# A planned schedule for windowed attention and two feed-forward networks: more word buffers, another cost model in the planner, other ranks

## The chip, the cores and the metric

One core of one Trainium2 chip runs the whole program in one launch. The metric is device time in microseconds (us), lower is better. The engines are TensorE (PE in the profile, PEld its weight loads), VectorE (DVE), ScalarE (ACT), GpSimd (POOL) and SyncE (SP), which issues nearly all transfers in program order.

## The reference

Inputs are float32. There are three parts, each fed by the one before:

```python
# attention: batch 4, 8 heads, 576 positions, head_dim 64
scores = q @ k^T / 8 - slope[head] * |i - j|      # only 0 <= i - j < 128
x = softmax(scores) @ v                           # -> 2304 tokens x 512
# first network: 512 -> 1024 -> 512
h = x @ w_in
solu = h * softmax(h)
ln = (solu - mean) / sqrt(var + 1e-6) * g_ln
x = ln @ w_out
# second network: 512 -> 1536 -> 512
g, val = x @ w_gate, x @ w_val
out = (g * sigmoid(g) * val) @ w_out2
```

## The kernel before, in words

**Attention** goes through 20 steps c (4 batches, 5 blocks of 128 query positions, the last of 64). A step has four units of two heads each. `load(c)` (line 380) fetches queries, keys and values; `score(c, qd)` (line 437) forms the scores of two units as small tiled products (line 463); `attend(u)` (line 484) adds the bias on VectorE (line 504), takes exponentials on ScalarE (lines 530 and 539), turns the result on TensorE (line 558), copies it to SBUF (lines 568 and 571) and multiplies it with the values, again as small tiled products (line 607). For steps c below `SUMS` (4, line 49) the division by the row sums comes after the product with the values: small products of the inverse sums with the identity (line 615) spread them, ScalarE or VectorE copies them (line 637), VectorE multiplies (line 640). For later steps each unit is normalized before it is turned (`invert`, lines 508 to 510, and `normalize`, lines 512 to 517). For steps below `WHOLE` (20, line 51) the products with the values come in two groups of two units, otherwise in one group of four (line 577).

**The first network** works on 18 tiles of 128 tokens: `up(i)` (line 716) is 24 products of 512 columns (line 712) and the statistics, `flip(i)` (line 778) turns the normed tile, and `down1(i)` (line 830) is another 24 products (line 712). For tiles in `FLIP_BY_DMA` (4 to 13, line 47) the turn is done by transfers: a copy splits the words in 16-bit halves (`halves_of`, line 261), a store writes them to memory and a turning transfer brings them back (line 258). Other tiles are turned by 8 TensorE transposes (line 817). Four buffers `e1` hold the exponentials until the turn is done.

**Weights** come as 64-bit words. `fetch` (line 289) takes one of the `DEC1[0]` = 4 buffers `dw` (line 38) and loads 512 KB; `unpack` (line 303) makes float32 of it with two ScalarE operations (lines 311 and 315), two VectorE operations (316 and 317) and an add on GpSimd (319), which gives the buffer back (line 321). Then the value is split in a high and a low part, and every dense product is the sum of three such products. `w_in` has 8 blocks, `w_out` 8. The second network has 36 more (`DEC2`).

**The second network** runs 36 steps of seven products (`products(s)`, line 1064, products in line 1083), in an order mostly written out by hand (`line`, lines 872 to 883), then the last product (`steps_of(k)`, line 1241, products in line 1262).

**The planner.** All of this is written as generators that yield operations. `Emitter.run` (line 199) plays them against a cost model and so fixes the program order of every engine: at each turn it takes the earliest time at which an engine can start an operation, and among that engine's operations that are ready at that time the one of lowest rank (lines 206 to 217). An operation with several ways (engines) goes where its end, plus a bias for VectorE and ScalarE (line 82), comes first. Ranks count tiles: a step's is its first token over 128, its loads come 0.5 earlier (line 1321), the up-projection of tile i has i + `LEAD`, the down-projection i + `LEAD` + `R_DOWN`; `PW_IN` and `PW_OUT` are ranks of the weight blocks, the `O_` constants offsets of single operations. What `dma` returns as its fifth entry is the time from the end of the issue to the landing (lines 254 to 259). For TensorE there is a rule on tiled operations (`form` 1 for scores, 2 for values, 0 for all else):

```python
if ops[0][4][0] == "PE" and first > TOGETHER:
    tiled = [x for x in ops if form(x)]
    if 0 < len(tiled) < len(ops) and not self.form:
        if len(tiled) < LEAST and min(x[3][2] for x in tiled) > first - PATIENCE:
            ops = [x for x in ops if not form(x)]
    elif tiled and self.form:
        same = [x for x in tiled if form(x) == self.form]
        ops = same or tiled
```

Here `first` is the time that can be had, `x[3][2]` the time at which an operation became ready, and `TOGETHER` 76077.562 ns. The planner's costs and dependences choose order and engine only; on the chip an instruction waits for the data and buffers that it uses.

Of the kernel before, what the change touches and what calls it, by code (L numbers as in the profile page):

```python
# [13 lines left out]
AF = mybir.ActivationFunctionType  # L14
# [7 lines left out]
DF1 = 1024  # L22
# [15 lines left out]
DEC1 = (4, 2)  # L38
# [8 lines left out]
FLIP_BY_DMA = range(4, 14)  # L47
PLB = 2
SUMS = 4
PTB = 4  # L50
WHOLE = 20
VDB = 3
PW_2 = -0.766
LEAD = 3.373
R_FLIP = 0.741
R_DOWN = 3.0
PW_IN = [-0.63, -0.31, -0.37, -0.36, 0.17, 0.09, 0.35, 0.2]
PW_OUT = 5.23
B_DVE = 1863.684
B_ACT = 700.0  # L60
HALVES = [(0, 1), (1, 0), (0, 0)]
HB = NC2 // 2
O_MAX = 0.338
O_EXP = -0.005
O_INV = 0.814
O_TURN = -0.064
O_PT = -1.188
O_VAL = 0.0
O_X = 0.674
O_SC = 0.33  # L70
O_DEC = 0.0
O_SPL = -0.05
O_FLIP = -1.299
O_LN = -0.345
O_SET = 0.102
O_FREE = -1.17
# [3 lines left out]
PATIENCE = 517.289  # L80
LEAST = 3
# [27 lines left out]
class Emitter:  # L109
# [4 lines left out]
    HOP = 90.0  # L114

    def __init__(self):
        self.busy, self.pending, self.count, self.open = {}, [], 0, {}
        self.now = 0.0
        self.form = 0

# [77 lines left out]

    def run(self):
        while self.pending:  # L200
# [17 lines left out]
            if engine == "PE":  # L218
                if first > TOGETHER and getattr(fn, "form", 0) != self.form:
                    cost += 95.0  # L220
                self.form = getattr(fn, "form", 0)
            self.pending.remove(op)
            fn()
            self.busy[engine.rstrip("+")] = t + cost
            if engine.endswith("+"):
                self.busy["+"] = t + cost
            op[5].settle(t + cost + self.HOP + op[4])
# [4 lines left out]
def attention_then_two_ffns(ctx: ExitStack, tc: tile.TileContext, qk, v, w_in, w_out, g_ln, w2, tables_d, out):  # L232
# [21 lines left out]
    def dma(dst, src, nbytes, deps=(), by=nc.sync):  # L254
        return (DMA, max(445.0, nbytes / 345.0), lambda: by.dma_start(dst, src), deps, 2000.0)

    def turn_by_dma(dst, src, nbytes, deps=()):
        return (DMA, 1000.0 + 1.56 * src.shape[0], lambda: nc.sync.dma_start_transpose(dst, src), deps,
                1300.0 + min(900.0, nbytes / 290.0))

    def halves_of(dst, src, n):
# [3 lines left out]
                (POOL, 450.0 + 0.3 * 2 * n, lambda: nc.gpsimd.tensor_copy(dst, words))]  # L265
# [19 lines left out]
    def decoder(pool, n, landing=2000.0):  # L285
        dec.update(pool=pool, n=n, dw=Slots(n[0]), db=Slots(n[1]), landing=landing)
# [16 lines left out]
    def unpack(d, words, got):  # L303
# [7 lines left out]
        r = yield (ACT, t_act(512), lambda: nc.scalar.activation(a, lw, AF.Copy, scale=2.0 ** -29), (), 0.0, O_DEC)  # L311
# [3 lines left out]
        x = yield (ACT, t_act(512), lambda: nc.scalar.activation(bf, hf, AF.Abs, scale=2.0 ** -112), (), 0.0, O_DEC)  # L315
# [3 lines left out]
        x = yield (POOL, t_pool(512), lambda: nc.gpsimd.tensor_tensor(  # L319
# [22 lines left out]
    decoder(at, DEC1)  # L342
# [37 lines left out]
    def load(c):  # L380
# [9 lines left out]
        for j in range(2) if c == 0 else (0,):  # L390
# [4 lines left out]
            if c == 0 and j == 0:  # L395
                chain((yield dma(tables, tables_d, 131072, (), nc.scalar)), base_ok)
                ident_ok.append((yield (DMA, 445.0, lambda: None, (), 2000.0)))
                tri_ok.append((yield (DMA, 445.0, lambda: None, (), 2000.0)))
# [85 lines left out]
    def attend(u):  # L484
# [18 lines left out]
        for j in range(2):  # L503
            d = yield (DVE, t_dve(P), lambda j=j: nc.vector.tensor_tensor_reduce(  # L504
# [32 lines left out]
        else:  # L537
            for j, d in enumerate(ds):
                ex.append((yield (ACT, 93 + t_act(P, True, True), lambda j=j: nc.scalar.activation(  # L539
                    e[0:n, j], e[0:n, j], AF.Exp, bias=st[0:n, j:j + 1], scale=-1.0,  # L540
                    accum_out=sc[0:n, j:j + 1]), [d, ds[0]], 0.0, O_EXP)))
            x = yield (DVE, 360, invert, ex, 0.0, O_INV)
            em.give(bank_s, x, k)
            x = yield ([(DVEP, t_dve(2 * P), lambda: normalize(nc.vector)),
                        (ACT, 2 * (93 + t_act(P)), lambda: normalize(nc.scalar)),
                        (POOL, t_pool(2 * P), lambda: normalize(nc.gpsimd))], [x], 0.0, O_INV)
# [47 lines left out]
        if c < SUMS and pr == NPAIR - 1:  # L594
            for r in range(NPAIR):
                yield summed[c * NPAIR + r]
            y = yield (DVE, 160, lambda: nc.vector.tensor_scalar_add(rs[c][0:n, 1], rs[c][0:n, 0], 1e-9), (), 0.0, O_INV)
            inv.append((yield (DVE, 190, lambda: nc.vector.reciprocal(rs[c][0:n, 2], rs[c][0:n, 1]), [y], 0.0, O_INV)))
# [777 lines left out]
```

## Time and profile before

| | us |
|---|---|
| median of 3 runs | 732.78 |
| lowest, highest | 731.4, 734.84 |
| the profiled execution, its own time | 732.14 |
| its span, first to last instruction | 730.3 |
| TensorE busy | 704.8 (97% of the span) |
| VectorE busy | 540.0 (74%) |
| ScalarE busy | 458.1 (63%) |
| GpSimd busy | 272.2 (37%) |

The busy share is an average over stages: attention and the first network fill the first 320 us or so, the second network the rest. Matmuls are pipelined and their ends are modelled, so the distance from one start to the next tells more than a duration. In a timeline the row gives the start, the length, the engine, the line, the operation and how many; idle time in front of it stands in brackets with what ended it.

### The profile page before, as it was taken

To read this page: it belongs to the slowest core of one execution; us is meant where nothing else is said; L and a number is where in the kernel's file an instruction comes from. 1 tells how busy PE (TensorE), PEld (TensorE's weight loads), DVE (VectorE), ACT (ScalarE), POOL (GpSimd) and SP (SyncE) were. 2 spreads that over 40 slices of the span, in tenths; PEclk is the share of its full clock that TensorE was granted. 3 is DMA by queue.
4 is the path that set the end of the run, shared out by engine and by line. 5 is a ranking of instruction groups with operands and counts; after the bars stand their busy time and mean duration, and the time that the engine had idled before them with its cause. 6 is when DMAs were issued, how large, how long until landed. Compare 5 with 4: busy or idle time off the path is not lost.

```text
span 730.3 us, 14535 instructions
## 1 busy us (share of the span) xinstructions
PE 704.8 (97%) x5148; PEld 635.2 (87%) x5148; DVE 540.0 (74%) x1480; ACT 458.1 (63%) x1127; POOL 272.2 (37%) x278
## 2 busy tenths in 40 slices
PE   5899899999999999999999999999999999999998
PEld 3567678777888888888899999999999999999997
DVE  6888985476566656988978767667775599886966
ACT  7899977777667775776647555655563574442532
POOL 3777776545675563550022412424221002110200
PEclk9999999999999999999999999999999999999999
DMA  8853325524454326256443454365541798886951
GB/s 289 249 168 109 103 73 146 167 89 116 133 151 109 94 75 173 73 145 148 150 170 131 151 169 163 125 188 190 184 151 66 263 360 307 254 299 203 300 177 66
DMA packets 92297, 121.86 MB, mean 167 GB/s; under 512 B 46400, under 2 KB 58688, under 8 KB 92224
## 3 DMA queue, kind: packets, MB, share of 16 engines
q1 hardware_dynamic: 91808, 120.48, 52.2%
q8 instruction: 40, 0.66, 0.4%
q10 hardware_dynamic: 416, 0.46, 0.2%
q14 instruction: 33, 0.27, 0.1%
HBM read 76.62 MB, written 34.34 MB: 152 GB/s over the span
## 4 chain that ended last, share of the span: by engine, by line
PE 76%; ACT 10%; DVE 9%; issue 2%; DMA 1%; POOL 1%; ACTq 0%; SPq 0%; DVEq 0%; POOLq 0%
PE bank L1083 31%; PE bank L712 21%; PE bank L1262 18%; PE bank L607 2%; ACT e L539 2%; PE bank L463 2%; PE bank L558 2%; ACT bank L754 1%; ACT pt L571 1%; ACT e L530 1%; DVE e L504 1%; PE bank L817 1%; DVE yt L277 1%; DMA tables<-tables 1%; DVE pt L568 1%
## 5 line engine op out<-in xcount | busy, mean ns | idle before, releaser
L1083 PE MATMUL bank<-yt,w 128*128 128x384 f32 x1008 | 186.3, 337 | 1.8 <-ACT t L1112 1.0
L1083 PEld LDWEIGHTS bank<-yt,w 128*128 128x128 f32 x1008 | 176.2, 188 | 4.1 <-ACT set L1110 1.5
L1262 PE MATMUL bank<-w,wo 128*128 128x384 f32 x756 | 133.1, 337 | 0.6 <-DVE set L1123 0.6
L319 POOL TENSOR_TENSOR db<-db,dw 128x512 int32<-128x512 int32 x52 | 73.2, 1409 | 161.2 <-DVE db L317 110.7
L1262 PEld LDWEIGHTS bank<-w,wo 128*128 128x128 f32 x756 | 132.4, 188 | 0.9 <-DVE set L1123 0.9
L712 PE MATMUL bank<-wout,lnT 128*128 128x512 f32 x432 | 102.5, 392 | 0.0
L1083 PE MATMUL bank<-shared,w 128*128 128x384 f32 x504 | 97.6, 337 | 0.0
L712 PEld LDWEIGHTS bank<-wout,lnT 128*128 128x128 f32 x432 | 80.4, 188 | 16.7 <-issue 0.2
L1083 PEld LDWEIGHTS bank<-shared,w 128*128 128x128 f32 x504 | 88.2, 188 | 1.1 <-ACT set L1110 0.5
L712 PE MATMUL bank<-shared,shared 128*128 128x512 f32 x288 | 79.8, 410 | 0.8 <-ACT shared L273 0.8
L712 PEld LDWEIGHTS bank<-shared,shared 128*128 128x128 f32 x288 | 52.2, 191 | 13.0 <-issue 1.9
L539 ACT ACTIVATE e<-e,st 128x128 f32<-128x128 f32 (+1 forms) x128 | 49.7, 402 | 21.5 <-DVE st L504 19.8
L273 ACT CAST w<-t 128x384 fp32r<-128x384 f32 (+2 forms) x35 | 26.6, 771 | 39.7 <-DVE t L1206 27.4
L504 DVE CUSTOM_DVE_ANT_0 e<-bank,bias 128x128 f32<-128x128 f32 (+1 forms) x160 | 38.2, 283 | 6.9 <-PE bank L463 5.0
L517 POOL TENSOR_TENSOR e<-e,st 128x256 f32<-128x256 f32 (+1 forms) x55 | 33.2, 618 | 21.9 <-ACT e L539 9.9
L277 DVE TENSOR_TENSOR w<-db,w 128x512 fp32r<-128x512 f32 (+1 forms) x46 | 31.4, 690 | 12.7 <-ACT w L273 12.4
L311 ACT ACTIVATE dw<-dw 128x512 int32<-128x512 uint32 x52 | 35.0, 675 | 7.0 <-DMA dw<-w 5.1
L316 DVE TENSOR_SCALAR db<-db 128x512 uint32<-128x512 uint32 x52 | 27.5, 532 | 16.0 <-ACT db L315 16.0
L273 ACT CAST w<-db 128x512 fp32r<-128x512 f32 (+1 forms) x48 | 26.9, 566 | 19.7 <-POOL db L319 9.4
L317 DVE SCALAR_TENSOR_TENSOR db<-dw,db 128x512 uint32<-128x512 uint32 x52 | 38.5, 744 | 0.8
L712 PE MATMUL bank<-shared 128*128 128x512 f32 x144 | 39.1, 394 | 0.0
L558 PE MATMUL bank<-tables,e 128*128 128x128 f32 x160 | 29.7, 293 | 9.0 <-ACT e L530 5.8
(124 smaller groups left out, 1242.7 us busy)
## 6 DMA issues: line engine op xcount, KB each, us to landing
dw<-w SPq DMA_DIRECT2D x36, 512.0 KB, 4.1
t<-ascr SPq DMA_DIRECT2D x21, 768.0 KB, 6.0
ascr<-set SPq DMA_DIRECT2D x34, 384.0 KB, 2.7
later<-ascr SPq DMA_DIRECT2D x15, 768.0 KB, 5.9
wo<-wscr SPq DMA_DIRECT2D x6, 896.0 KB, 7.2
v<-v SPq DMA_DIRECT2D x20, 256.0 KB, 3.6
lscr<-pl SPq DMA_DIRECT2D x20, 256.0 KB, 2.4
raw<-qk SPq DMA_DIRECT2D x19, 256.0 KB, 4.0
```

What stands on the lines that cost most here:

```text
L273: return [(ACT, t_act(n, sbuf), lambda: nc.scalar.copy(hi, src)), (DVEP if sbuf else DVE, t_dve(n, sbuf), lambda: nc.vector.tensor_copy(hi ...
L277: ways = [(DVEP if sbuf else DVE, t_dve(n), lambda: nc.vector.tensor_sub(lo, src, hi.bitcast(F32)))]
L311: r = yield (ACT, t_act(512), lambda: nc.scalar.activation(a, lw, AF.Copy, scale=2.0 ** -29), (), 0.0, O_DEC)
L317: x = yield (DVEP, t_dve(512), lambda: nc.vector.scalar_tensor_tensor(b, hw, 0x80000000, b, ALU.bitwise_and, ALU.bitwise_or), [x], 0.0, O_DEC)
L319: x = yield (POOL, t_pool(512), lambda: nc.gpsimd.tensor_tensor(b.bitcast(I32), b.bitcast(I32), a, ALU.add), [x, r], 0.0, O_DEC)
L504: d = yield (DVE, t_dve(P), lambda j=j: nc.vector.tensor_tensor_reduce(e[0:n, j], sc[0:n, j * 256:j * 256 + P], bias[0:n, 2 * pr + j, bs], ...
L517: eng.tensor_tensor(e[0:n], e[0:n], st[0:n, 6:8].unsqueeze(2).to_broadcast([n, 2, P]), ALU.mult)
L539: ex.append((yield (ACT, 93 + t_act(P, True, True), lambda j=j: nc.scalar.activation(e[0:n, j], e[0:n, j], AF.Exp, bias=st[0:n, j:j + 1], ...
L558: nc.tensor.transpose(tp[:, j], e[:, j], ident)
L712: nc.tensor.matmul(o, terms[m][0], terms[m][1], start=(m == 0), stop=(m == len(terms) - 1))
L1083: nc.tensor.matmul(o, l, r, start=first and m == 0, stop=m == 5, skip_group_check=True)
L1262: nc.tensor.matmul(o, w[:, b], ob[k, i][a][:, j], start=i == 0 and m == 0, stop=i == HB - 1 and m == 2)
```

## The change

It raises the word buffers of the first decode from 4 to 8, SUMS from 4 to 6, and FLIP_BY_DMA by tiles 2 and 3; it lowers WHOLE from 20 to 9; it changes the costs of many operations in the planner; it gives the planner one transfer pipe that all transfers share, a clock of TensorE that is at half pace after a rest, and a time of its own for each engine from the end of an operation to the start of what depends on it; and it sets new ranks and offsets. The core of the diff:

```diff
-DEC1 = (4, 2)
+DEC1 = (8, 2)
-FLIP_BY_DMA = range(4, 14)
+FLIP_BY_DMA = range(2, 14)
-SUMS = 4
+SUMS = 6
-WHOLE = 20
+WHOLE = 9
-PW_2 = -0.766
-LEAD = 3.373
-R_FLIP = 0.741
-R_DOWN = 3.0
-PW_IN = [-0.63, -0.31, -0.37, -0.36, 0.17, 0.09, 0.35, 0.2]
-PW_OUT = 5.23
-B_DVE = 1863.684
-B_ACT = 700.0
+PW_2 = -7.666
+LEAD = 3.482
+R_FLIP = 0.643
+R_DOWN = 3.05
+PW_IN = [-2.377, -0.384, -0.272, -0.324, 0.113, -0.017, 0.254, -0.253]
+PW_OUT = 4.216
+B_DVE = 2121.667
+B_ACT = 1450.719
-O_MAX = 0.338
-O_EXP = -0.005
-O_INV = 0.814
-O_TURN = -0.064
-O_PT = -1.188
-O_VAL = 0.0
-O_X = 0.674
-O_SC = 0.33
-O_DEC = 0.0
-O_SPL = -0.05
-O_FLIP = -1.299
-O_LN = -0.345
-O_SET = 0.102
-O_FREE = -1.17
+O_MAX = 0.83
+O_EXP = 0.472
+O_INV = -1.063
+O_TURN = -2.17
+O_PT = -3.394
+O_VAL = 0.51
+O_X = 0.204
+O_SC = -0.291
+O_DEC = 0.631
+O_SPL = 0.292
+O_FLIP = -1.182
+O_LN = -0.959
+O_SET = 1.858
+O_FREE = -3.54
-PATIENCE = 517.289
-LEAST = 3
+PATIENCE = -358.533
+LEAST = 8
+WARM, COOL = 3400.0, 1900.0
...
-    HOP = 90.0
+    HOP = {"PE": 170.0, "ACT": 130.0, "DVE": 100.0, "POOL": 60.0, "DMA": 0.0}
...
+    def paced(self, t, cost):
+        gap = t - self.warmed
+        if gap > COOL or self.rest and gap > 400.0:
+            self.rest = WARM
+        slow = min(2 * cost, self.rest)
+        self.rest -= slow
+        cost += slow / 2
+        self.warmed = t + cost
+        return cost
...
             if engine == "PE":
-                if first > TOGETHER and getattr(fn, "form", 0) != self.form:
-                    cost += 95.0
+                if self.form and not getattr(fn, "form", 0):
+                    cost += 100.0
                 self.form = getattr(fn, "form", 0)
+                cost = self.paced(t, cost)
             self.pending.remove(op)
             fn()
+            if engine == "DMA":
+                self.busy[engine] = t + min(cost, 420.0)
+                self.pipe = max(t + 2300.0, self.pipe) + cost
+                op[5].settle(self.pipe + op[4])
+                continue
...
     def dma(dst, src, nbytes, deps=(), by=nc.sync):
-        return (DMA, max(445.0, nbytes / 345.0), lambda: by.dma_start(dst, src), deps, 2000.0)
+        return (DMA, nbytes / 360.0, lambda: by.dma_start(dst, src), deps, 400.0)
...
-                (POOL, 450.0 + 0.3 * 2 * n, lambda: nc.gpsimd.tensor_copy(dst, words))]
+                (POOL, 980.0, lambda: nc.gpsimd.tensor_copy(dst, words))]
...
-    decoder(at, DEC1)
+    decoder(at, DEC1, 700.0)
...
-                    accum_out=sc[0:n, j:j + 1]), [d, ds[0]], 0.0, O_EXP)))
-            x = yield (DVE, 360, invert, ex, 0.0, O_INV)
+                    accum_out=sc[0:n, j:j + 1]), ds, 0.0, O_EXP)))
+            x = yield (DVE, 280, invert, ex, 60.0, O_INV)
...
-            for p in pieces(h[q], terms, 6, 233.0):
+            for p in pieces(h[q], terms, 6, 227.0):
...
-            return (PE, 6 * 0.461 * NH, f, deps)
+            return (PE, 6 * 0.4525 * NH, f, deps)
```

The hunks left out change only planner's costs and the time after an operation, in the same way.

## Rows read from the trace of the kernel before

**Rows 1.** The page, busy us of each engine over the span.

```profile
PE 704.8 (97%) x5148; PEld 635.2 (87%) x5148; DVE 540.0 (74%) x1480; ACT 458.1 (63%) x1127; POOL 272.2 (37%) x278
```

**Rows 2.** Busy time by stretch: stretch, its length, engines, granted clock, DMA share, GB/s.

```profile
0.00:30.00 30.00, 17.95 (x255) 10.96 (x255) 20.83 (x89) 23.07 (x70) 15.82 (x17) 0.94 0.84 279
30.00:120.00 90.00, 83.91 (x872) 64.41 (x872) 75.27 (x308) 79.38 (x251) 68.68 (x73) 0.98 0.39 118
120.00:300.00 180.00, 178.54 (x1636) 143.47 (x1635) 113.23 (x505) 125.36 (x392) 99.54 (x117) 1.00 0.45 123
300.00:580.00 280.00, 278.14 (x1557) 271.04 (x1557) 208.20 (x383) 163.78 (x322) 74.04 (x64) 1.00 0.48 154
580.00:731.00 151.00, 146.30 (x834) 145.34 (x832) 122.50 (x199) 66.47 (x96) 14.09 (x9) 1.00 0.73 249
```

**Rows 3.** Waits of TensorE, 0 to 30: total, times, longest.

```profile
PE bank L558 <- ACT e L530: 5.8, 7, 1.8
PE bank L463 <- DMA raw<-qk: 5.5, 1, 5.5
```

**Rows 4.** Timeline of TensorE around 92 us.

```profile
91.32 0.77 PE L463 MATMUL bank<-keys,raw 64*32 64x160 f32 x30 [1.93 <-DVE shared L277]
92.02 3.46 PE L712 MATMUL bank<-shared,shared 128*128 128x512 f32 x8
95.28 1.36 PE L712 MATMUL bank<-shared 128*128 128x512 f32 x4
```

**Rows 5.** The chain that ended last, in order of time: start, us, what.

```profile
32.87 0.87 PE bank L615 x16
...
230.02 9.75 PE bank L712 x42
239.77 0.87 PE bank L558 x8
```

**Rows 6.** Busy time by stretch, 90 to 100.

```profile
90.00:100.00 10.00, 8.68 (x88) 6.78 (x88) 7.33 (x37) 8.22 (x29) 8.75 (x11) 0.83 0.28 79
```

**Rows 7.** Waits of SP's queue, 0 to 30.

```profile
SPq L255 <- POOL db L319: 8.0, 4, 2.7
```

**Rows 8.** Timeline of SP, the eighth transfer of w_in.

```profile
24.13 0.33 SPq L255 DMA_DIRECT2D dw<-w_in  x1
```

**Rows 9.** The page's DMA issues: count, KB each, median us to landing.

```profile
dw<-w_in SPq DMA_DIRECT2D x8, 512.0 KB, 4.7
```

**Rows 10.** Busy time by stretch, 0 to 14.

```profile
0.00:14.00 14.00, 5.83 (x78) 3.03 (x78) 9.95 (x46) 10.14 (x32) 3.44 (x8) 1.00 0.87 307
```

**Rows 11.** Timeline of GpSimd, the decode of w_in, first and last instruction.

```profile
7.30 1.29 POOL L319 TENSOR_TENSOR db<-db,dw 128x512 int32<-128x512 int32 x1 [0.68 <-ACT bias L413]
...
45.37 1.27 POOL L279 TENSOR_TENSOR shared<-db,shared 128x512 fp32r<-128x512 f32 x1 [1.24 <-ACT shared L273]
```

**Rows 12.** Timeline of TensorE, the scores of step 1.

```profile
18.69 2.29 PE L463 MATMUL bank<-keys,raw 64*32 64x160 f32 x64
```

**Rows 13.** The copies in halves on GpSimd: ns min/median/max, first and last start.

```profile
L265 POOL COPY pl<-e x18: 1033/1044/1053, 112.8 to 260.9; 128x1024 uint16<-128x1024 uint16 x18
```

**Rows 14.** Timeline of TensorE around 227 us.

```profile
225.04 1.64 PE L712 MATMUL bank<-shared,shared 128*128 128x512 f32 x6
226.61 0.44 PE L607 MATMUL bank<-pt,vd 128*64 128x128 f32 x4
...
229.41 0.39 PE L607 MATMUL bank<-pt,vd 128*64 128x128 f32 x4
229.63 0.39 PE L607 MATMUL bank<-pt,v 128*64 128x128 f32 x4
229.95 0.73 PE L712 MATMUL bank<-shared,shared 128*128 128x512 f32 x2
```

**Rows 15.** Timeline of TensorE, 55 to 78, first and last of the tiled groups.

```profile
55.70 0.34 PE L607 MATMUL bank<-pt,vd 128*64 128x64 f32 x4
...
77.29 0.77 PE L463 MATMUL bank<-keys,raw 64*32 64x160 f32 x32
```

## What was predicted

> **What bounds the kernel now.** I read the page's busy shares first, then busy time by stretch, then what TensorE waited for, then the order of its instructions where it is full and where it is not. TensorE is busy 704.8 of 730.3 us [rows 1], so idle time can give back 25 us at most. By stretch [rows 2] TensorE is idle for 12.0 us in the first 30, for 6.1 from 30 to 120, for 1.5 from 120 to 300, for 1.9 from 300 to 580, and for some 4 at the end, which is the last sums and their store. So from 120 us on TensorE is the bound, and only what takes work off it helps there. Before that the three elementwise engines set the pace: from 30 to 120 ScalarE is busy 79.4, VectorE 75.3 and GpSimd 68.7 of 90 us. The waits of the first 30 us [rows 3] say what TensorE lacks: 5.5 us are the first query block on its way, and 5.8 us in seven pieces are softmax exponentials, which stand in ScalarE's queue among decodes of weights. Idle time has a second price: after the wait of 1.93 us at 91.3 the next eight dense products take 3.26 us, from 92.02 to 95.28 [rows 4], where eight of the 42 back to back take 1.86 (9.75/42 is 232 ns each [rows 5]). The granted clock of that stretch is 0.83 [rows 6], between the levels of 1.2 and 2.4 GHz, and 1.4 us are lost.
>
> **What of the change reaches the chip.** Costs, due times and ranks are numbers of the planner; they change only the order of instructions and which of two or three engines takes an operation. The longer list of dependences of the exponentials is a planner's as well; the chip waits for data only. Four constants change instructions: the word buffers, SUMS, FLIP_BY_DMA and WHOLE.
>
> **Eight word buffers.** Today the fifth w_in transfer and those after it wait for a buffer, which GpSimd's add returns: SP waits 8.0 us for it in the first 30 us [rows 7], and the eighth transfer is issued at 24.13 [rows 8]; with 4.7 us to landing (median of the eight [rows 9]) it is there at 28.8. With eight buffers all eight are issued at the start, since their ranks (-2.377 to 0.254) lie below the 0.5 of step 1's loads. In front of and with them go 0.79 MB of step 0 and 0.33 MB of tables: 5.31 MB. The DMA engines moved 307 GB/s over the first 14 us [rows 10]; at that rate it is all there at 17.3, some 11 us sooner. GpSimd's share of the decode is two instructions of 1.3 us for each block, the first at 7.30 and the last at 45.37 [rows 11]; sixteen of these and the five others in the stretch, at 1.3 each, fill 27 us, so it could end near 35 instead of 46.6. The first up-projection can then be whole some 10 us sooner, and TensorE has dense work while attention waits.
> The cost: step 1's query and key blocks (0.52 MB) now stand behind the weights and arrive at about 5.83 MB / 307 GB/s = 19.0, where its scores run at 18.69 today [rows 12]. I add 0.8 for the landing; bounds 0 and 2.5 (the value block and one landing more). Later steps' blocks are not later than today's, as the bytes ahead of them are the same.
>
> **What can be recovered.** The exponential waits (5.8), the idle of 30 to 120 (6.1) and the stretch at the lower clock (1.4) make 13.3 us. Bounds: nothing, and all of it. I take two thirds, -8.9, since the transfers' share of the cause goes entirely while ScalarE, busy for 88% of 30 to 120, goes on limiting; the new order moves decode behind the exponentials (its offset rises from 0 to 0.631) and the larger bias keeps flexible copies off ScalarE.
>
> **SUMS from 4 to 6.** Two more steps have their sums spread by TensorE: 16 small products each at 54 ns (0.87/16 [rows 5]), +1.7 us where TensorE is nearly full. The eight normalizations that go are work of the three elementwise engines beside the path, and part of the two thirds.
>
> **FLIP_BY_DMA from tile 2.** Two tiles lose 8 transposes each at about 0.109 us (0.87/8, the same shape [rows 5]): -1.7. They gain four copies of 1.04 us (GpSimd [rows 13]), four stores and four turning transfers on SP. The DMA engines are 39% busy from 30 to 120 [rows 2], which hides the transfers; a down-projection is ranked 3.05 tiles behind its up-projection, which hides the delay. Without that cover it is the up-projections that wait, four tiles later, for the exponentials' buffers.
>
> **WHOLE from 20 to 9.** In eleven steps the products with the values run in one group where two stood. Where the tiled groups end costs about 0.10 us (0.32 from the last four small products to the next dense one, 0.22 from four to four [rows 14]); one such end less in each is -1.1; bounds 0 and -3 (a whole entry and exit each, next).
>
> **No holding back.** After 76 us the planner of before lets tiled operations wait until three are ready or one has waited 517 ns. With a patience of -358 the condition can never hold (an operation that is ready was ready before now plus 358), so each tiled operation goes as soon as its rank allows. Around 225 us a step's values and both scores stand in one group [rows 14]. Its entry costs 0.18 (1.57 us from the first of six dense products to the first tiled one; six at 232 ns are 1.39), its end 0.10: 0.28 us. Ahead of 76 us, where nothing is held today, I count six such groups from 55.7 to 77.3 [rows 15] for about two steps. Thirteen steps lie behind 76 us. I take half a group more for each, since ranks that lie close bring many together and one that is ready joins a group already begun: +1.8. Bounds 0 and two more each, +7.3.
> The Trainium skill (TensorEngine Tiling (Array Packing), Tiling Modes) says that changing the tiling mode drains TensorE; the trace agrees, with the 0.28 us of [rows 14] as its price. By that rule the meeting of scores and values, which are tiled differently, pays as well, and separate groups cost less than they seem: the term would lie nearer its lower bound.
>
> **Everything else** (ranks of the second network, evacuations later, sums earlier): 0. TensorE idles only 1.9 us from 300 to 580, and dense products cover any reordering of ScalarE, 58% busy there. Bounds -1.9 and, as much lost again, +1.9.
>
> **Sum:** -8.9 + 0.8 + 1.7 - 1.7 - 1.1 + 1.8 = -7.4. The profiled execution took 732.14 us (its span of 730.3 and 1.8 around it); less 7.4 is 724.7. The median of the runs is 0.6 higher, 732.78; that gives 725.3, and I predict 725.0.
>
> **Rivals.** (1) **The elementwise engines hold the pace anyway.** For it: ScalarE's 88%; the decode's work is not less, and w_out's follows at once. Against: VectorE and GpSimd have 15 and 21 us free from 30 to 120. Then some 4 of the 13.3 come back and one more group per step costs 13 x 0.28 = 3.6: 732.8 - 4 + 3.6 = 732. No change; chance 0.20.
> (2) **Tiled groups fall apart** in the full stretch behind 76 us. For it: the six groups ahead of 76 us; the new planner prices an exit at 100 ns and an entry at nothing, where the trace has 0.28 for the two. Against: WHOLE joins values from step 9 on. With three more groups in each of 13 steps the price is 39 x 0.28 = 10.9; it decides when 0.28 for each group exceeds what startup recovers by 3.7, at a third recovered (4.4) from 29 groups on. Then 732.8 - 4.4 + 10.9 = 739. Slower; chance 0.16.
> The drain at each change of mode is the Trainium skill's rule of that page.
> (3) **Startup closes fully:** all 13.3, no new groups, WHOLE at its best: 732.8 - 13.3 - 3 = 716; it needs decode off ScalarE entirely in the first 30 us, where that engine is busy 23.1. Chance 0.14.
> The forecast has 0.50, by itself 719 to 729.
>
> **Chances and range.** A measurement of this kernel tells about 0.5% from no change: below 729.1 is faster, above 736.4 slower. Faster is the forecast and (3), 0.64; the same is (1), 0.20; slower is (2), 0.16. The range from 715 to 738 takes in (3), the forecast and (1), and leaves out the far half of (2) and the tails.
>
> **What would show it.** Right: all eight w_in transfers issued before 8 us and no wait of SP for GpSimd's add among them; the last w_in split before 40 instead of 46.6; more dense products by 60 us; TensorE idle below 4 from 30 to 120; 96 small sums products and 48 transposes of the normed tiles. Wrong: scores of step 1 after 21 us; the exponential waits undiminished; more than 13 further tiled groups after 76 us; new TensorE waits behind 300 us.

## The result, and the profile after

The changed kernel takes 724.41 us (median of 6 runs, 724.17 to 726.25), the kernel before 731.46 beside it (6 runs, 730.5 to 734.84): a ratio of 0.9904, 95% interval 0.9887 to 0.9921. The forecast was 725.0. The number held, but its largest term did not: TensorE gained nothing in the first 90 us, where 8.9 us had been expected, and the gain came from stretches that the sum had put at nothing or little.

The page of the changed kernel, busy us of each engine; TensorE is busy 5.2 us less than in [rows 1], and all others but GpSimd are busy less as well:

```profile
PE 699.6 (97%) x5164; PEld 631.4 (87%) x5164; DVE 536.0 (74%) x1460; ACT 453.8 (63%) x1115; POOL 287.4 (40%) x291
```

Busy time by stretch of the changed kernel, to be read beside [rows 2]:

```profile
0.00:30.00 30.00, 16.33 (x253) 10.37 (x260) 20.03 (x84) 25.37 (x84) 15.62 (x17) 1.00 0.97 324
30.00:120.00 90.00, 86.81 (x1008) 64.79 (x991) 76.51 (x317) 79.03 (x252) 71.08 (x74) 1.00 0.42 126
120.00:300.00 180.00, 178.54 (x1556) 143.64 (x1555) 120.06 (x498) 122.39 (x369) 108.47 (x124) 1.00 0.50 131
300.00:580.00 280.00, 279.64 (x1583) 275.29 (x1581) 202.00 (x380) 167.42 (x326) 79.55 (x69) 1.00 0.50 162
580.00:723.00 143.00, 138.32 (x786) 137.34 (x786) 117.38 (x186) 59.56 (x86) 12.64 (x9) 1.00 0.70 237
```

In the first 30 us TensorE is idle for 13.7 us, more than the 12.0 of before, and ScalarE is busier. From 30 to 120 it is idle for 3.2 instead of 6.1. From 120 to 300 it is as busy as before, so a gain there has to be less time for the same work, not less idle time. The waits of TensorE in the first 30 us, beside [rows 3], say that the exponentials hold it longer than before:

```profile
PE bank L576 <- ACT e L548: 7.6, 7, 3.2
PE bank L481 <- DMA raw<-qk: 5.2, 1, 5.2
```

The transfers did what was forecast. SP's timeline has seven of the w_in transfers in one row (the first of the eight is issued at 0.72), and only then step 1's queries; the eighth of before was issued at 24.13 [rows 8]:

```profile
3.09 4.97 SPq L273 DMA_DIRECT2D dw<-w_in  x7
8.11 0.48 SPq L273 DMA_DIRECT2D raw<-qk  x1
```

The decode did not. GpSimd's timeline has the last low part of w_in at 45.78, where [rows 11] had it at 45.37:

```profile
45.78 1.28 POOL L297 TENSOR_TENSOR shared<-db,shared 128x512 fp32r<-128x512 f32 x1 [1.12 <-ACT shared L291]
```

The scores of step 1 came 0.6 us later than in [rows 12], as forecast:

```profile
19.28 2.39 PE L481 MATMUL bank<-keys,raw 64*32 64x160 f32 x64
```

Busy time cannot show where 8 us came from, since TensorE is full nearly everywhere. What can is the work it has done by a given time: each product counted at what it takes back to back (0.232 us for 512 columns and 0.109 for a transpose, both from [rows 5]; 0.054 for a product with values or sums of 128 columns and 0.03 for one of 64, 0.020 for a score, and 0.175 for the 384 columns of the second network, from the starts in full stretches). The table was counted so from the traces, one execution of each kernel:

```
us of TensorE's work started by the time at the left
        before  changed  difference
  90      57.9     58.1      +0.2
 120      82.3     84.7      +2.5
 200     156.0    161.8      +5.8
 300     254.0    258.9      +4.9
 340     292.9    298.9      +6.0
 380     331.4    339.0      +7.6
 400     351.0    359.2      +8.2
 700     650.4    658.6      +8.2
```

So nothing by 90 us, 2.3 from 90 to 120, 2.4 from 120 to 300 (3.3 by 200, of which 0.9 is lost again), 3.3 from 300 to 400, and nothing more: 8.2 us of work against spans that differ by 7.9 (730.3 and 722.4).

The 2.4 us of 120 to 300 are not fewer waits: waits of over 0.1 us put products off by 2.3 us there before and by 2.6 after. What fell is the number of times that TensorE changes between dense products, scores and products with values: 48 times before, 33 in the changed kernel. By the starts and the prices above, the products at these places come late by 6.7 us in sum before (one at a wait left out) and by 4.6 after.

### The profile page after: what moved, and what is told of

Read it like the earlier page. It is cut to its first block, busy times and chain, and to the rows that moved or that the text cites. A ratio compares the mean times of both kernels' runs of the same rounds, so it can differ in the third digit from the quotient of the medians.

```text
span 722.4 us, 14538 instructions
## 1 busy us (share of the span) xinstructions
PE 699.6 (97%) x5164; PEld 631.4 (87%) x5164; DVE 536.0 (74%) x1460; ACT 453.8 (63%) x1115; POOL 287.4 (40%) x291
## 4 chain that ended last, share of the span: by engine, by line
PE 79%; DVE 9%; ACT 7%; issue 2%; POOL 2%; DMA 1%; SPq 0%; ACTq 0%; POOLq 0%; DVEq 0%
PE bank L1101 35%; PE bank L730 22%; PE bank L1280 14%; PE bank L625 2%; PE bank L481 2%; PE bank L576 2%; DVE w L295 2%; DVE wo L295 1%; ACT e L557 1%; ACT e L548 1%; ACT pt L589 1%; ACT dw L329 1%; DMA tables<-tables 1%; PE bank L835 1%; DVE t L1224 1%
## 5 line engine op out<-in xcount | busy, mean ns | idle before, releaser
L337 POOL TENSOR_TENSOR db<-db,dw 128x512 int32<-128x512 int32 x52 | 70.8, 1362 | 133.6 <-DVE db L335 70.0
L730 PE MATMUL bank<-wout,lnT 128*128 128x512 f32 x432 | 105.3, 395 | 0.0
L730 PEld LDWEIGHTS bank<-shared,shared 128*128 128x128 f32 x288 | 50.7, 189 | 11.9 <-issue 3.1
L557 ACT ACTIVATE e<-e,st 128x128 f32<-128x128 f32 (+1 forms) x112 | 43.7, 400 | 11.8 <-DVE st L522 8.5
L576 PE MATMUL bank<-tables,e 128*128 128x128 f32 x160 | 32.7, 295 | 10.8 <-ACT e L548 8.1
L576 PEld LDWEIGHTS bank<-tables,e 128*128 128x128 f32 x160 | 20.3, 143 | 25.7 <-ACT e L548 13.1
L1135 ACT ACTIVATE set<-set 128x384 f32<-128x384 f32 x34 | 17.7, 525 | 35.4 <-DVE set L1133 35.2
L1225 POOL TENSOR_TENSOR t<-t 128x384 f32<-128x384 f32 x4 | 5.9, 1468 | 84.7 <-DMA t<-ascr 52.4
L589 ACT COPY pt<-bank 128x256 f32<-128x256 f32 (+1 forms) x80 | 26.5, 354 | 20.7 <-DVE pt L586 10.9
```

What stands on the lines that cost most here:

```text
L337: x = yield (POOL, 1290, lambda: nc.gpsimd.tensor_tensor(b.bitcast(I32), b.bitcast(I32), a, ALU.add), [x, r], 0.0, O_DEC)
L557: ex.append((yield (ACT, 68 + t_act(P, True, True), lambda j=j: nc.scalar.activation(e[0:n, j], e[0:n, j], AF.Exp, bias=st[0:n, j:j + 1], ...
L576: nc.tensor.transpose(tp[:, j], e[:, j], ident)
L589: ys.append((yield ([(ACT, t_act(w, False), lambda: nc.scalar.copy(pt[:, 0, :, 0:n], tp[:, :, 0:n])), (DVE, t_dve(w), lambda: nc.vector.te ...
L730: nc.tensor.matmul(o, terms[m][0], terms[m][1], start=(m == 0), stop=(m == len(terms) - 1))
```

## The experiments

Every edit of a constant makes the planner plan anew, and the order can change everywhere behind the first difference. The kernels are therefore read by the same count of work, against the changed kernel, until the first place where they fall back. The change's own order with fewer word buffers was not tried. All times below are medians; each ratio is to the kernel before on the same chip.

```
us of TensorE's work started by the time at the left
      changed second_old whole20 hold lead350 copy_first  dw4 dw4_found four_old_found db4_new
  90     58.1       57.9    58.1  56.1    57.9       58.1  52.1      57.6           60.1    58.6
 120     84.7       84.7    84.5  83.1    84.7       85.0  80.2      83.8           87.0    84.5
 200    161.8      161.8   159.2 160.1   160.3      160.4 157.5     156.0          161.1   160.1
 300    258.9      258.9   255.9 257.0   257.5      257.7 254.5     252.4          257.1   256.1
 340    298.9      298.9   296.3 296.5   297.5      297.5 294.6     292.6          297.1   296.3
 380    339.0      335.5   332.2 332.6   331.9      337.1 334.7     332.7          335.4   336.4
 580    539.4      535.9   532.9 533.4   532.7      537.8 535.5     532.5          536.3   536.9
 700    658.6      654.6   651.8 652.1   651.2      657.5 654.2     651.4          652.9   655.6
```

### Constants alone, planner and ranks alone

**four_new**, the kernel before with the four new constants and everything else old:

```diff
-DEC1 = (4, 2)
+DEC1 = (8, 2)
-FLIP_BY_DMA = range(4, 14)
+FLIP_BY_DMA = range(2, 14)
-SUMS = 4
+SUMS = 6
-WHOLE = 20
+WHOLE = 9
```

> The kernel before, its planner and its ranks, with the four constants that change instructions (word buffers 8, SUMS 6, WHOLE 9, FLIP_BY_DMA from tile 2). Theory A: these are worth little by themselves, within 2 us of the kernel before on either side. Theory B: most of the gain is there, 5 us or more faster, and the last low part of w_in is split 5 us or more ahead of 46.6.

Measured: 738.17 us, ratio 1.0091, interval 1.0068 to 1.0113: 6.2 us slower than the kernel before, outside both theories. The last low part of w_in starts at 43.98, 1.4 us sooner than before and not 5. **four_old**, the changed kernel with these four put back:

> The changed kernel, its planner and its ranks, with the four constants of the kernel before. Theory A: most of the gain stays, at most 3 us slower than the changed kernel. Theory B: most of it goes, 5 us or more slower.

Measured: 733.91 us, ratio 1.0027, interval 1.0013 to 1.004, which is theory B's side. Neither half gives the gain: the constants alone cost 0.9%, planner and ranks alone 0.3%. Two parts that each make the kernel slower and together make it 1% faster do not add up as terms of a sum.

### The second network's ranks

**second_old**, the changed kernel with the three ranks that matter only to the second network put back:

```diff
-PW_2 = -7.666
+PW_2 = -0.766
-O_SET = 1.858
+O_SET = 0.102
-O_FREE = -3.54
+O_FREE = -1.17
```

> The changed kernel with three of the planner's numbers as before: PW_2, O_SET and O_FREE, which rank only work of the second network. Theory A (the gain has several places, and some 3.5 us of it lie between 330 and 400 us, where TensorE of the kernel before waits at the start of the second network): 2.5 to 4 us slower than the changed kernel, 727 to 728.5, and a wait of TensorE of 0.5 us or more returns between 320 and 365. Theory B (the forecast: startup gives nearly all, through the word buffers and less idling before 120 us): within 1 us of the changed kernel, since startup is untouched.

Measured: 729.68 us, ratio 0.9972, interval 0.9959 to 0.9984. In the table it is the changed kernel up to 340 us and 3.5 behind at 380, and changes little after that (0.5 us by 700). Theory A's place is right, and waits return there (0.77 us at 353.5 for a y part, 1.09 at 357.5 for a copy of line 1128); the loss, some 5 us, is more than its 2.5 to 4. Theory B fell. **second_new**, the three new ranks in the kernel before:

> The kernel before with the new PW_2, O_SET and O_FREE alone. Theory A: 2.5 to 4 us faster than the kernel before, 727.5 to 729, the waits between 328 and 363 gone. Theory B: the same as before within 1 us.

Measured: 730.81 us, ratio 0.999, interval 0.9977 to 1.0003: nothing that can be told from noise, as theory B said. TensorE still waits 1.9 us from 300 to 400, as long as in the kernel before. The same three numbers are worth 0.7% in one plan and nothing in another.

### One number of the changed kernel at a time

**whole20**:

```diff
-WHOLE = 9
+WHOLE = 20
```

> The changed kernel with WHOLE 20 again: values in two groups of two units in all steps. Forecast's term: 1.1 us slower (0 to 3). Theory C: 2 to 5 us slower.

Measured: 731.65 us, ratio 1.0007, interval 0.9994 to 1.0019. Two separate losses stand in the table: 2.8 us between 120 and 300, and 4.2 more between 340 and 380. Most of the first goes with the constant. Busy time of whole20 in that part:

```profile
120.00:200.00 80.00, 78.81 (x755) 61.23 (x754) 52.04 (x244) 52.06 (x181) 52.93 (x64) 1.00 0.54 148
200.00:280.00 80.00, 79.63 (x680) 62.97 (x679) 51.82 (x209) 46.73 (x151) 44.51 (x53) 1.00 0.42 108
```

And of the changed kernel:

```profile
120.00:200.00 80.00, 79.24 (x762) 63.37 (x761) 50.70 (x243) 54.57 (x184) 52.06 (x62) 1.00 0.57 150
200.00:280.00 80.00, 79.30 (x699) 63.56 (x698) 50.66 (x216) 52.83 (x160) 44.99 (x54) 1.00 0.46 121
```

TensorE is busy for 158.4 and 158.5 us, at the full clock, and has done 2.8 us less in whole20 (the table's 3.0 at 300 less the 0.2 it was behind at 120). It changes 46 times between dense products, scores and values from 120 to 300 where the changed kernel does 33 times, and by the starts these places cost 1.9 us more; the rest is spread. The size is not certain to the tenth: lead350 below, with WHOLE at 9 and 32 such changes, loses 1.4 us in the same stretch. The second loss is told under lead350.

**hold**, the waiting for tiled operations put back:

```diff
-PATIENCE = -358.533
-LEAST = 8
+PATIENCE = 517.289
+LEAST = 3
```

> The changed kernel with PATIENCE 517.289 and LEAST 3, so that tiled operations are held back after 76 us again. Forecast's term: 0.28 us a group, some 6 groups more, so 1.8 us faster than the changed kernel. Theory C (each plan is found for its numbers, and any number changed alone costs some us): 2 to 5 us slower, whatever the count of tiled groups does.

Measured: 730.47 us, ratio 0.9988, interval 0.9974 to 1.0002. From 120 to 300, where holding could help, it does 173.9 us of work and the changed kernel 174.2 (the table's differences): no gain from holding is seen there, where the forecast's term asked for 1.8. It loses 1.6 us before 120 and 4.0 between 340 and 380.

**dw4**:

```diff
-DEC1 = (8, 2)
+DEC1 = (4, 2)
```

> The changed kernel with 4 word buffers for the first decode, planned anew. Theory A (the buffers bring w_in sooner but no decode sooner, since ScalarE and the order set the decode): the last low part of w_in is split within 3 us of the changed kernel's 47.1, and any loss against 724.4 is one of planning, spread behind 50 us, up to 5 us. Theory B (the buffers carry the gain at startup): the last low part 5 us or more later, TensorE's work by 120 us 5 us or more behind.

Measured: 727.8 us, ratio 0.9949, interval 0.9929 to 0.9969. It is 6.0 us behind at 90 and 4.5 at 120. The rows of TensorE there show one stall and slow small products after it, at a granted clock of 0.50 from 77.5 to 80 us (16 take 1.98 us, where the changed kernel's row at 41.64 has 16 in 1.09):

```profile
73.56 0.66 PE L625 MATMUL bank<-pt,v 128*64 128x128 f32 x8
77.54 1.98 PE L633 MATMUL bank<-tables,rs 128*64 128x128 f32 x16 [3.32 <-DVE rs L616]
```

This wait is for VectorE's inverse sums (line 616), not for a weight. With four buffers the decode itself is no later, as theory A said: GpSimd's row of dw4 has the last low part of w_in at 45.15, where the changed kernel has it at 45.78:

```profile
45.15 1.27 POOL L297 TENSOR_TENSOR shared<-db,shared 128x512 fp32r<-128x512 f32 x1 [1.07 <-ACT shared L291]
```

And dw4 is the one of these four that does not stall near 350 us, which is why it ends before the others in spite of its start.

**lead350**, a change of a rank by 0.018 of a tile, to see what any new plan costs:

```diff
-LEAD = 3.482
+LEAD = 3.50
```

> The changed kernel with LEAD 3.50 instead of 3.482: ranks of the first network later by 0.018 tiles, some 0.3 us of TensorE's time, which means nothing by itself but changes the order of some operations. Theory C: 2 to 5 us slower than the changed kernel, as much as the runs that undid a part. If single parts of the change carry the gain, this one is within 1 us of the changed kernel.

Measured: 730.69 us, ratio 0.9994, interval 0.9983 to 1.0004. A number that stands for nothing takes the whole gain back. By their ratios hold, lead350 and whole20 are 6.1 to 7.5 us slower than the change, more than theory C's 2 to 5. Up to 120 us the work of lead350 is the same, by 340 it is 1.4 behind, and at 380 7.1. TensorE in lead350 just there:

```profile
355.02 0.62 PE L1101 MATMUL bank<-yt,w 128*128 128x384 f32 x2 [0.89 <-ACT yt L291]
356.02 1.85 PE L1101 MATMUL bank<-yt,w 128*128 128x384 f32 x9 [0.37 <-DVE yt L295]
360.00 12.28 PE L1101 MATMUL bank<-yt,w 128*128 128x384 f32 x60 [2.14 <-ACT set L1128]
```

Three waits, the last for the copy of a PSUM bank (line 1128). ScalarE in lead350 shows that copy in its queue:

```profile
354.14 1.77 ACT L291 CAST yt<-t 128x768 fp32r<-128x768 f32 x2 [2.88 <-DVE t L1053]
...
356.18 0.69 ACT L329 ACTIVATE dw<-dw 128x512 int32<-128x512 uint32 x1
357.39 0.52 ACT L1127 ACTIVATE set<-set 128x384 f32<-128x384 f32 x1 [0.53 <-DVE set L1125]
357.82 0.64 ACT L333 ACTIVATE db<-dw 128x512 f32<-128x512 f32 x1
358.37 0.66 ACT L329 ACTIVATE dw<-dw 128x512 int32<-128x512 uint32 x1
358.94 0.66 ACT L333 ACTIVATE db<-dw 128x512 f32<-128x512 f32 x1
359.50 0.45 ACT L1128 COPY set<-bank 128x384 f32<-128x384 f32 x1
```

Four decode operations of weights, for which TensorE waits nowhere from 350 to 400 us, stand in front of a copy that TensorE needs at once. The changed kernel has the copy ahead of the decode:

```profile
353.60 0.48 ACT L1128 COPY set<-bank 128x384 f32<-128x384 f32 x1 [0.91 <-PE bank L1101]
...
355.01 0.66 ACT L329 ACTIVATE dw<-dw 128x512 int32<-128x512 uint32 x1
```

In this execution the wait costs twice. Busy time by stretch of lead350:

```profile
350.00:360.00 10.00, 6.59 (x35) 5.63 (x33) 8.79 (x16) 5.76 (x11) 0.21 (x1) 1.00 0.36 134
360.00:370.00 10.00, 10.00 (x48) 10.00 (x49) 4.48 (x10) 2.70 (x6) 3.25 (x3) 0.83 0.44 146
```

3.4 us idle, and then 48 products in 10 us of full work at a granted clock of 0.83 (0.50, the lower of its two levels, from 362 to 364). The second part is not in every execution. whole20 has the same three waits (0.77, 0.42 and 2.21 us; here is the last) and 1.00 behind them:

```profile
361.25 11.06 PE L1101 MATMUL bank<-yt,w 128*128 128x384 f32 x62 [2.21 <-ACT set L1128]
```

```profile
360.00:370.00 10.00, 8.75 (x50) 8.75 (x51) 6.50 (x13) 3.95 (x9) 3.49 (x3) 1.00 0.42 142
```

Of the ten executions of lead350, five have a granted clock of 0.998 or less over the whole span, with a median of 731.35 us, and five have 0.999 or 1.0, with 729.65. The waits for line 1128 are 2.2 us in whole20, hold and four_old as well, and 1.1 in second_old; the changed kernel and dw4 have none.

### The stall alone

**copy_first**, lead350 with the offset of these copies lowered, so that they stand before most of the decode:

```diff
 LEAD = 3.50
-O_SET = 1.858
+O_SET = -1.0
```

> The changed kernel with the up-projections' rank at 3.50 instead of 3.482, as in lead350, and with the offset of the PSUM copies of the second network at -1.0 instead of 1.858. In ScalarE's program the copy that TensorE waited 2.14 us for at 360 us in lead350 then stands in front of three of the four decode operations (0.66 us each) that it stood behind, while the softmax, the y parts and the steps before it keep their order. Theory S1, the copy behind the decode makes the stall: the wait of the product for that copy falls from 2.14 to under 0.8 us, no stretch of a lower granted clock follows it, and 3 to 4 us come back: 726.5 to 728. Rival S2, the y parts that come late on VectorE and ScalarE make it: TensorE waits as long for yt or another copy within 350 to 365, and the time stays at 729.5 to 731.5.

Measured: 724.79 us, ratio 0.9911, interval 0.9894 to 0.9928, where lead350 had 0.9994: the changed kernel's time is back, 5.9 us (the ratios differ by 0.8%) where S1 had 3 to 4. Against the five executions of lead350 with 0.999 or 1.0 it is still 4.9 us. TensorE and then ScalarE of copy_first in the same place:

```profile
352.52 1.73 PE L1101 MATMUL bank<-yt,w 128*128 128x384 f32 x9
354.67 17.66 PE L1101 MATMUL bank<-yt,w 128*128 128x384 f32 x100 [0.42 <-DVE yt L295]
```

```profile
354.94 0.69 ACT L329 ACTIVATE dw<-dw 128x512 int32<-128x512 uint32 x1
355.52 0.46 ACT L1128 COPY set<-bank 128x384 f32<-128x384 f32 x1
```

And its busy time in the second stretch, 59 products where lead350 had 48:

```profile
360.00:370.00 10.00, 10.00 (x59) 10.00 (x59) 5.40 (x9) 3.87 (x9) 2.03 (x2) 1.00 0.59 184
```

By the table copy_first and lead350 are equal at 340, 5.2 apart at 380 and 6.3 at 700: 3.0 of it is the idle time of 350 to 360 (3.4 and 0.4), 1.9 the eleven products at 0.175. That the stall near 355 us, and not the nudge elsewhere, took most of the gain is shown. S1's signs came: no wait for that copy, and no lower clock. Which of the stall's parts counts is not shown: the new offset also brought VectorE's y parts forward (the waits for yt fell from 1.26 to 0.42 us), so S1 and S2 are not told apart; the copy's place accounts for the longest wait of the three.

### The old constants with ranks found for them

**dw4_found** and **four_old_found** ask whether the constants or the ranks carry the gain:

```diff
-DEC1 = (8, 2)
+DEC1 = (4, 2)
...
-LEAD = 3.482
+LEAD = 3.457
...
-O_SET = 1.858
+O_SET = 4.641
...
```

> The changed kernel with four word buffers instead of eight, and with ranks and offsets that were found for this constant by a random search against the planner's own end time, from those of the change; SUMS, WHOLE and FLIP_BY_DMA as in the change. Theory C (the gain belongs to a plan found against the new cost model, whichever constants it was found for): 723.5 to 726.5, as the change itself. Rival B (the eight buffers carry the gain that dw4, at 727.8, lacked): 727 to 730, with TensorE 3 us or more behind the change by 90 us.

Measured: 730.52 us, ratio 0.9988, interval 0.9977 to 1.0. Both sides miss. By 90 us it is 0.5 behind the change and by 120 0.9, so four buffers were enough for the start; yet it loses 4.9 more by 200. One stall makes most of it, in TensorE's row, with 0.68 as the granted clock of the five us in which it ends (two views of dw4_found):

```profile
145.86 1.83 PE L576 MATMUL bank<-tables,e 128*128 128x128 f32 x6 [3.24 <-POOL e L535]
```

```profile
145.00:150.00 5.00, 3.88 (x12) 2.76 (x13) 1.27 (x3) 2.03 (x4) 4.99 (x7) 0.68 0.89 185
```

GpSimd's queue before it:

```profile
139.04 2.54 POOL L297 TENSOR_TENSOR lnT<-e,lnT 128x512 fp32r<-128x512 f32 x2
141.56 1.52 POOL L789 TENSOR_SCALAR e<-e,mst 128x512 f32<-128x512 f32 x2
143.02 2.21 POOL L283 COPY pl<-e 128x1024 uint16<-128x1024 uint16 x2
145.20 2.32 POOL L535 TENSOR_TENSOR e<-e,st 128x256 f32<-128x256 f32 x4
```

Four normalizations whose inverse sums were ready at 142.34 stand behind the two copies in halves for a turn by transfer. The planner had chosen GpSimd for both.

> The changed kernel with all four constants of before (four word buffers, SUMS 4, WHOLE 20, tiles 4 to 13 turned by transfers), and with ranks and offsets found for them by the same random search against the planner's end time. Every product, copy and transfer is then one that the kernel before has; order and engines alone differ from it. Theory C: 724 to 727.5, so that at least two thirds of the change's 8 us come without its four constants. Rival B (the four constants carry the gain; four_old at 733.9 was slower because it lacked them): 730.5 or more.

Measured: 730.12 us, ratio 0.999, interval 0.9974 to 1.0006: theory C's number is missed, rival B's bound almost met. The table says otherwise than rival B, though. With all four old constants this kernel is 2.0 us ahead of the change at 90 and 2.3 at 120. It loses 4.1 from 120 to 300 (WHOLE is 20 again, and TensorE changes 54 times between dense products, scores and values where the changed kernel does 33 times), 1.8 from 340 to 380, and 2.6 from 580 to 700, where two weights come late in the second network:

```profile
616.07 3.36 PE L1280 MATMUL bank<-w,wo 128*128 128x384 f32 x18 [1.21 <-DVE w L295]
620.13 30.14 PE L1280 MATMUL bank<-w,wo 128*128 128x384 f32 x171 [0.70 <-DVE w L295]
```

The last two, 4.4 us where it is 5.7 behind at 700, lie in a stage that none of the four constants touches; the 4.1 lie where WHOLE acts. So this kernel settles neither theory.

**db4_new**, more buffers behind the word buffers:

```diff
-DEC1 = (8, 2)
+DEC1 = (8, 4)
...
-LEAD = 3.482
+LEAD = 3.485
...
```

> The changed kernel with four buffers behind the word buffers (DEC1 of (8, 4) instead of (8, 2)), and with ranks found for it by the same random search. Theory D (the two db buffers hold the decode of w_in, so that eight word buffers could not speed it): the last w_in split on GpSimd ends its start below 42 us instead of 45.78, and TensorE is 2 us or more ahead of the change by 60 us; 720 to 723. Rival E (ScalarE and GpSimd are full in that stretch): the split stays at 44 to 47, and the time at 723.5 to 726.5 by the plan alone.

Measured: 727.21 us, ratio 0.9945, interval 0.9927 to 0.9963. Theory D falls. The last split is later, in GpSimd's row of db4_new, and TensorE is not ahead by 60:

```profile
50.57 1.27 POOL L297 TENSOR_TENSOR shared<-db,shared 128x512 fp32r<-128x512 f32 x1
```

Rival E's time is missed by 0.7 us, so it isn't shown either. What sets the end of w_in's decode stays open: fewer word buffers (dw4, 45.15) did not put it off and more buffers behind them did not bring it forward, each in an order of its own.

## Why the prediction was right, and where it was not

**The number was right by terms that were wrong, so its closeness is luck.** Of the signs named ahead, the transfers, the idle time from 30 to 120 and the counts said right. The last w_in split said wrong, and so did the dense products by 60 us (46, before 48) and the exponential waits. Point by point:

- **Eight word buffers (the first up-projection 10 us sooner): failed.** All eight transfers were issued by 8.1 us, but the decode ended 0.4 us later than before. The step that failed is the one from transfers to decode: GpSimd's share was costed at full use, though its instructions come behind ScalarE's. ScalarE was busy 25.4 of 30 us. The trace shows its decode operations spread between exponentials and copies, the last of line 333 at 42.35.
- **What can be recovered (-8.9): failed.** The exponential waits went from 5.8 to 7.6 and nothing was gained by 90 us. 2.3 us came from 90 to 120, where the 1.93 us wait of [rows 4] and the lower clock behind it are gone. The first 90 us look as rival (1) has them, with the elementwise engines holding the pace; its number, 732, was wrong.
- **Step 1's scores (+0.8): held**, 0.6 measured.
- **SUMS and FLIP_BY_DMA (+1.7, -1.7): the counts held.** In the groups of the changed kernel's instructions there are 96 small sums products (64 before) and 48 transposes (64 before):

```profile
L835 PE MATMUL bank<-ident,e 128*128 128x128 f32 x48 | 6.6, 274 | 0.0
L633 PE MATMUL bank<-tables,rs 128*64 128x128 f32 (+1 forms) x96 | 6.0, 268 | 1.2 <-DVE rs L616 1.2
```

- **WHOLE (-1.1, bounds 0 and -3): mis-sized.** whole20 puts it at -2.8 from 120 to 300, near the far bound. Over eleven steps that is 0.25 each, near the 0.28 of a whole group with entry and end, as the bound assumed, and not the 0.10 of an end alone. As lead350 loses 1.4 in that stretch without the constant, the size is rough; 1.9 of it stands at the places where the form changes.
- **No holding back (+1.8, bounds 0 and +7.3): mis-sized.** With the holding put back, the stretch from 120 to 300 does 0.3 us less work, not more: about 0. There are 20 tiled groups behind 76 us, 17 before. WHOLE hides a part of it: whole20 has 24, so the count of six or seven more was near. The price is what the rows put in doubt: scores and values that meet inside a group pay too, so a further group can cost less than its 0.28. From a product with values to a score 0.20 us pass and from a score to one with values 0.23 (medians from 120 to 300 of the kernel before), where products of the same form follow at 0.054 and 0.020 on average. By the Trainium skill (TensorEngine Tiling (Array Packing), Tiling Modes), changing the tiling mode drains TensorE; these rows agree. A closer size than about 0 is not shown, since lead350's nudge moves the same stretch by 1.4. Rival (2) needed 29 more groups.
- **Everything else (0, bounds -1.9 and +1.9): failed.** The change gained 3.3 us from 300 to 400, more than the bound. TensorE idled there for 1.9 us before; I took that as all there was to get and dense products as cover for any reordering of ScalarE. It was not all. Counted from start to start, the products of the kernel before come 3.2 us late in sum from 300 to 400, those of the changed kernel not at all. Idle time is counted from a product's modelled end, 337 ns after its start, while the next could start after 175, so each wait costs some 0.16 us more than it reads. And the start of the second network lacks the cover: each of a step's later products waits for the copy of a bank that an earlier one filled. The kernel before stalls for two such copies, 0.99 and 0.41 us, and 0.34 for a y part. The longest, first TensorE, then ScalarE of the kernel before, with a load of an activation table in front of the copy:

```profile
326.48 4.34 PE L1083 MATMUL bank<-yt,w 128*128 128x384 f32 x24
331.81 9.07 PE L1083 MATMUL bank<-yt,w 128*128 128x384 f32 x48 [0.99 <-ACT t L1112]
```

```profile
329.27 1.28 ACT L1109 ACT_TABLE_LOAD   x1
330.56 0.52 ACT L1109 ACTIVATE t<-t 128x384 f32<-128x384 f32 x1
330.99 0.39 ACT L273 CAST w<-db 128x256 fp32r<-128x256 f32 x1
331.29 0.47 ACT L1112 COPY t<-bank 128x384 f32<-128x384 f32 x1
```

The changed kernel has no TensorE wait from 300 to 400, and the same stretch runs without a break:

```profile
326.88 7.72 PE L1101 MATMUL bank<-yt,w 128*128 128x384 f32 x42
334.43 2.26 PE L1101 MATMUL bank<-shared,w 128*128 128x384 f32 x12
```

**Put together:** forecast -7.4; measured by stretch -0.2, -2.3, -2.4 and -3.3, in sum -8.2. **What the runs settle:** the gain has two kinds. The 2.4 us of 120 to 300 go mostly with fewer changes between forms, and these with WHOLE (whole20 has 46); the 5.6 of 90 to 120 and 300 to 400 come where waits of the kernel before are gone, in one order of the queues. lead350 and copy_first show that a single stall, at a place that no constant of the change aims at, makes a difference of 5.9 us between two plans, where the whole gain is 7. **What they do not settle:** how much of the gain the new planner's numbers deserve. Theory C in its plain form, that any plan found by this planner does as well, fell with dw4_found and four_old_found: their ranks were found by the planner's end time, and on the chip they had stalls of 3.2 us (GpSimd's queue) and 1.2 (a weight from VectorE). No kernel here beats the change; copy_first equals it.

## What to carry to other kernels

In a kernel whose main engine is 97% busy, look for the gain of a reordering by counting the work done by a given time, stretch by stretch; busy shares and totals of waits hide both the small tiled products and the stretches at a lower granted clock. A single operation that stands in an in-order queue behind work nobody waits for can cost as much as a whole change brings: find the longest wait left, look at what runs ahead of its releaser, and move that. Before crediting a part of a plan made by a search, move an unrelated number by a hair; if the time moves as much, the part has not been measured.

## What the runs showed that was not expected

**The clock behind a wait.** A wait of TensorE of 2.14 us was followed by ten us at a mean granted clock of 0.83 (lead350), one of 3.24 us by 0.68 over five us (dw4_found), and one of 3.32 us by 0.50 over two and a half (dw4). Waits of 2.2 us left it at 1.00 in whole20, hold and four_old, and so did waits of 1.21 and 0.70 us in four_old_found. The wait of 1.93 us at 91 us of the kernel before had 0.83 behind it [rows 6]; in second_new, whose TensorE has the same order there, a wait of 1.93 us stands at the same place, and the stretch has 1.00:

```profile
90.00:100.00 10.00, 8.11 (x92) 6.00 (x92) 9.37 (x42) 9.09 (x33) 9.22 (x11) 1.00 0.28 79
```

So the same wait can have the lower clock behind it or not, and no run here shows what decides. The 1.4 us that the prediction put down for it are not there in every execution, and a part of the 2.3 us of 90 to 120 is of this kind.

**How far a hair moves the time.** 0.018 of a tile in one rank changed the time by 0.9%, as much as the change itself, and did so through orders that have done the same work by 120 us.
